# A retention layer with a feed-forward stage: one more load and cast buffer, and the first score group moved to the end of the previous head pair

## The chip, the cores and the metric

The kernel runs on one core of one Trainium2 chip. The time is device microseconds of one execution on that core, and the median of several executions is compared. The engines named below are PE (TensorE: matmuls, transposes and, as "PEld", their weight loads), DVE (VectorE), ACT (ScalarE), SP (SyncE, which here only issues DMAs) and POOL (GpSimd, which here does four memsets at the start).

## What is computed

The input is q, k and v of 4 batches, 8 heads, 768 positions and 64 channels, in fp32, and two weight matrices of 512 x 2048 and 2048 x 512.

```python
gamma = 1.0 - 2.0 ** (-5.0 - np.arange(H))
for t in range(S):
    state = gamma * state + einsum('bhd,bhe->bhde', k[:, :, t], v[:, :, t])
    y[:, :, t] = scale * einsum('bhd,bhde->bhe', q[:, :, t], state)
x = y.transpose(0, 2, 1, 3).reshape(B * S, H * D)
h = x @ w_in
g = h * tanh(log1p(exp(h)))
out = g @ w_out
```

The recurrence over positions is done in chunks of 128: inside a chunk with masked scores, across chunks with a 64 x 64 state for each head.

## The kernel before

There are two stages, one after the other. The first is the retention ("attention" in the names), for 16 head pairs: 4 batches times 4 pairs of heads, `it` = 0 to 15. The second is the feed-forward stage (lines 229 to 264), for 12 blocks of 256 tokens. The retention leaves its result in SBUF, in `xt`, where the second stage reads it.

For one head pair the first stage does this (the letters are used in the rest of the text):

- load: six DMAs of 192 KB, q, k and v of each head (lines 112, 115, 118), into a buffer set of the pool `rn_aload`, which has 3 sets. For the first eight pairs a weight DMA of 1 MB follows each load (`weight_piece`, lines 90 and 96). All DMAs are issued by SP.
- casts, on ACT: qp and kd for the first head, qp and kd for the second head (lines 131 and 134, fp32 to fp16 with a scale), then kb and vb for both heads (lines 137 and 138). They go to the pool `rn_acast`, which has 2 sets.
- QT and KT, on PE: six transposes of qp (line 142) and six of kb (line 144), each followed by a copy from PSUM to SBUF on DVE (lines 148 and 149).
- S.0 and S.1, on PE: the scores of chunks 0 to 2 and of chunks 3 to 5, six matmuls each (line 179), into one PSUM tile `at2`, of which there is a single buffer. AM.0 and AM.1, on DVE: the product of that tile with the mask (line 183).
- for each of the six chunks c: u (line 197, the chunk's k-v product), Y.c (line 199, masked scores times v), t.c (lines 202 and 205, the state's part of the result, one matmul for each head) on PE, and st.c on DVE (line 210, the new state). The result tile `yt_ps` in PSUM holds three chunks and has a single buffer.
- xt.0 after chunk 2 and xt.1 after chunk 5, on ACT: two copies each (lines 216 and 220) that bring `yt_ps` to SBUF. Y of the next three chunks can't start before the second of them has read the tile.

In the source, the loop body issues the load for pair `it`+2, then a weight piece, then casts, QT and KT for pair `it`+1, then everything else for pair `it`. The order on each engine's queue is not that of the source: when the kernel is built, a scheduler places the instructions on the queues by costs of its own, and what it makes is fixed before the run. Each engine then takes its instructions strictly in that order. After the fourth and the eighth weight piece, ACT casts a whole weight matrix to fp16 (lines 92 and 98).

The second stage computes, for each block, `hT` by 64 matmuls (line 242, copied out at line 246), Exp, Ln and Tanh on ACT (lines 249 to 251), the product `gt` on DVE (line 253) and the output by 32 matmuls (line 257), which go out by line 261 and a DMA.

Of the kernel before, what the change touches and what calls it, by code (L numbers as in the profile page):

```python
# [9 lines left out]
FP16 = mybir.dt.float16  # L10
FP32 = mybir.dt.float32
AF = mybir.ActivationFunctionType
ALU = mybir.AluOpType
# [3 lines left out]
def kernel(  # L17
# [9 lines left out]
    nc = tc.nc  # L27
# [3 lines left out]
    P = 128  # L31
    C = 128
    NCH = S // C
    HP = H // 2
# [37 lines left out]
    msk = cpool.tile([P, H, C], FP32)  # L72
# [9 lines left out]
    with tc.tile_pool(name="rn_wstage", bufs=1) as wstage:  # L82
      wtmp = wstage.tile([P, NBP, d_ff], FP32)
      wtmp2 = wstage.tile([P, NFB, d_model], FP32)
      win_ap = moe_w_in.rearrange("(bp p) f -> p bp f", p=P)
      wout_ap = moe_w_out.rearrange("(fb p) c -> p fb c", p=P)

      def weight_piece(j):
          if j < NBP:
              nc.sync.dma_start(wtmp[:, j], win_ap[:, j])  # L90
              if j == NBP - 1:
                  nc.scalar.copy(win16, wtmp)  # L92
          elif j < NBP + 4:
              jj = j - NBP
              fsl = slice(jj * (NFB // 4), (jj + 1) * (NFB // 4))
              nc.sync.dma_start(wtmp2[:, fsl], wout_ap[:, fsl])
              if jj == 3:
                  nc.scalar.copy(wout16, wtmp2)

      with tc.tile_pool(name="rn_aload", bufs=3) as lpool, \  # L100
         tc.tile_pool(name="rn_acast", bufs=2) as castp, \
         tc.tile_pool(name="rn_atp", bufs=2) as tpp, \
         tc.tile_pool(name="rn_asmall", bufs=3) as smallp, \
         tc.tile_pool(name="rn_apsum", bufs=1, space=bass.MemoryType.PSUM) as aps:

        def load(b, hp):
            hA = 2 * hp
            q2 = lpool.tile([P, NCH, 2, D], FP32, tag="q2")
            k2 = lpool.tile([P, NCH, 2, D], FP32, tag="k2")
            v2 = lpool.tile([P, NCH, 2, D], FP32, tag="v2")  # L110
            for hh in range(2):
                nc.sync.dma_start(
                    q2[:, :, hh],
                    q[b, hA + hh].rearrange("(c p) d -> p c d", p=P))
                nc.sync.dma_start(
                    k2[:, :, hh],
                    k[b, hA + hh].rearrange("(c p) d -> p c d", p=P))
                nc.sync.dma_start(
                    v2[:, :, hh],
                    v[b, hA + hh].rearrange("(c p) d -> p c d", p=P))  # L120
            return q2, k2, v2

        def prep(b, hp, loaded):
            hA = 2 * hp
            q2, k2, v2 = loaded
            qp2 = castp.tile([P, NCH, 2, D], FP16, tag="qp2")
            kb2 = castp.tile([P, NCH, 2, D], FP16, tag="kb2")
            vb2 = castp.tile([P, NCH, 2, D], FP16, tag="vb2")
            kd2 = castp.tile([P, NCH, 2, D], FP16, tag="kd2")
            for hh in range(2):  # L130
                nc.scalar.activation(  # L131
                    qp2[:, :, hh], q2[:, :, hh], AF.Copy,
                    scale=dvec[:, hA + hh:hA + hh + 1])
                nc.scalar.activation(
                    kd2[:, :, hh], k2[:, :, hh], AF.Copy,
                    scale=kdv[:, hA + hh:hA + hh + 1])
            nc.scalar.mul(kb2[:], k2[:], BOOST)
            nc.scalar.mul(vb2[:], v2[:], BOOST)
            qt_ps = aps.tile([P, S], FP16, tag="qt_ps")
            kt_ps = aps.tile([P, S], FP16, tag="kt_ps")  # L140
            for c in range(NCH):
                nc.tensor.transpose(  # L142
                    qt_ps[:, c * C:(c + 1) * C], qp2[:, c], ident)
                nc.tensor.transpose(  # L144
                    kt_ps[:, c * C:(c + 1) * C], kb2[:, c], ident)
            qt = tpp.tile([P, S], FP16, tag="qt")
            kt = tpp.tile([P, S], FP16, tag="kt")
            nc.vector.tensor_copy(qt, qt_ps)  # L148
            nc.vector.tensor_copy(kt, kt_ps)  # L149
            return qt, kt, vb2, kd2  # L150

        NIT = B * HP
        loads = [load(0, 0), load(0, 1)]
        pre = prep(0, 0, loads[0])
        for it in range(NIT):
            b, hp = divmod(it, HP)
            hA = 2 * hp
            qt, kt, vb2, kd2 = pre
            if it + 2 < NIT:
                nb, nhp = divmod(it + 2, HP)  # L160
                loads.append(load(nb, nhp))
            weight_piece(it)
            if it + 1 < NIT:
                nb, nhp = divmod(it + 1, HP)
                pre = prep(nb, nhp, loads[it + 1])
            tstate = smallp.tile([P, P], FP16, tag="tstate")
            nc.vector.memset(tstate, 0.0)
            HCH = NCH // 2
            yt_ps = None
            mskb = msk[:, hA:hA + 2].unsqueeze(2).broadcast_to(  # L170
                (P, 2, HCH, C))

            def qk_mask_group(g):
                at2 = aps.tile([P, 2, 4, C], FP32, tag="at2")
                for cc in range(HCH):
                    cs_ = slice((g * HCH + cc) * C, (g * HCH + cc + 1) * C)
                    for hh in range(2):
                        o = 64 * hh
                        nc.tensor.matmul(  # L179
                            at2[:, hh, cc], kt[o:o + 64, cs_],  # L180
                            qt[o:o + 64, cs_], start=True, stop=True)
                am = smallp.tile([P, 2, HCH, C], FP16, tag="atm")
                nc.vector.tensor_tensor(  # L183
                    am, at2[:, :, 0:HCH], mskb, op=ALU.mult)
                return am

            atm3 = qk_mask_group(0)
            atm3_next = None
            for c in range(NCH):
                cs = slice(c * C, (c + 1) * C)  # L190
                g, cc = divmod(c, HCH)
                if cc == 0:
                    yt_ps = aps.tile([P, HCH, 2, C], FP32, tag="yt_ps")
                if cc == 1 and g + 1 < NCH // HCH:
                    atm3_next = qk_mask_group(g + 1)
                u_ps = aps.tile([P, P], FP32, tag="u_ps", bufs=2)
                nc.tensor.matmul(
                    u_ps, kd2[:, c], vb2[:, c], start=True, stop=True)
                nc.tensor.matmul(  # L199
                    yt_ps[:, cc], vb2[:, c], atm3[:, :, cc],  # L200
                    start=True, stop=True)
                nc.tensor.matmul(  # L202
                    yt_ps[0:64, cc, 0], tstate[0:64, 0:64], qt[0:64, cs],
                    start=False, stop=True, skip_group_check=True)
                nc.tensor.matmul(  # L205
                    yt_ps[64:128, cc, 1], tstate[64:128, 64:128],
                    qt[64:128, cs], start=False, stop=True,
                    skip_group_check=True)
                tnew = smallp.tile([P, P], FP16, tag="tstate")
                nc.vector.scalar_tensor_tensor(  # L210
                    tnew, tstate, gcc[:, hp:hp + 1], u_ps,
                    op0=ALU.mult, op1=ALU.add)
                tstate = tnew
                if cc == HCH - 1:
                    c0 = c - HCH + 1
                    nc.scalar.copy(  # L216
                        xt[0:64, b, hp, c0 * C:(c + 1) * C].rearrange(
                            "p (c i) -> p c i", i=C),
                        yt_ps[0:64, :, 0])
                    nc.scalar.copy(  # L220
                        xt[64:128, b, hp, c0 * C:(c + 1) * C].rearrange(
                            "p (c i) -> p c i", i=C),
                        yt_ps[64:128, :, 1])
                    atm3 = atm3_next

    ntok = 0
    GF = 4
    with tc.tile_pool(name="rn_mh", bufs=2) as mhp, \
# [4 lines left out]
        for b in range(B):  # L233
            for cb in range(NCB):
                ts_all = slice(cb * CB, (cb + 1) * CB)
                hT = mhp.tile([P, NFB, CB], FP32)
                for gg in range(NFB // GF):
                    h4 = mps.tile([P, GF, CB], FP32, tag="h4", bufs=3)
                    for j in range(GF):
                        fb = gg * GF + j  # L240
                        for bp in range(NBP):
# [3 lines left out]
                                start=(bp == 0), stop=(bp == NBP - 1))  # L245
# [51 lines left out]
```

## Time and profile before

| what | value |
|---|---|
| median of 6 runs | 392.64 us (391.7 to 395.03) |
| the profiled execution | 393.51 us |
| its span, from the first to the last instruction | 391.7 us |
| mean granted TensorE clock over the span | 0.943 |
| first stage, from the start to the last xt copy | 0 to 170.86 us |
| second stage | 170.9 us to the end |
| first KT transposes of pair 0, 1, 2, 3 | 11.82, 20.56, 29.32, 40.84 us |
| first KT transposes of pair 10, 11, 12, 13, 14, 15 | 118.31, 125.98, 134.83, 144.14, 152.97, 161.73 us |
| weight casts on ACT (lines 92 and 98) | 7.0 us each, at 64.43 and 108.49 us |

The profiled execution lies 0.87 us above the median of the runs. A row of the "windows" view gives a stretch of the span in us, its length, the busy time of PE, PEld, DVE, ACT and POOL in it (with the number of instructions), the granted TensorE clock, the busy share of the DMA engines (as the view gives it; it can exceed 1) and the GB/s moved. A row of the timeline gives start, duration, engine, line, operation and tiles, and in brackets the idle time before it with what ended it. Buffer numbers in names (qp_359) tell the instances of a tile apart.

### The profile page before, as it was taken

Reading aid. Unit: us, or ns where it says so; the run is one execution under the profiler, and the core shown is the slowest. Engines: PE = TensorE matmul, PEld = TensorE weight load, DVE = VectorE, ACT = ScalarE, POOL = GpSimd, SP = SyncE. Lnnn points to the kernel's source line nnn. Section 1 sums busy time; section 2 is a strip of 40 time slices with the busy share of each in tenths; the row PEclk is TensorE's granted clock in tenths of the full one; section 3 lists DMA queues with packets and bytes.
Section 4 is the critical chain, followed back from the end, with each engine's and each line's share of the span. In section 5 each row is a group of like instructions: output and inputs, shape, how many; then the busy total and the mean of one; then the engine's idle time right before and its main releaser. Section 6 shows DMA issues by size and latency. Waiting matters only on the chain.

```text
span 391.7 us, 4763 instructions
## 1 busy us (share of the span) xinstructions
PE 299.1 (76%) x1920; PEld 172.8 (44%) x1920; DVE 204.9 (52%) x260; ACT 265.1 (68%) x223; POOL 0.2 (0%) x4
## 2 busy tenths in 40 slices
PE   0686666576658887889569979979996996995666
PEld 0342333233224444458426756564682665463222
DVE  0454444363445665527267485565837656483351
ACT  2664448855498765415993995799499399849920
POOL 0000000000000000000000000000000000000000
PEclk9999999999999999999959989998996998799589
DMA  8999999983458810000001101000010110001011
GB/s 172 218 278 261 289 266 245 258 210 80 92 122 173 169 23 0 2 0 2 0 0 55 54 2 54 33 22 28 27 55 0 54 55 0 28 36 44 2 54 54
DMA packets 82149, 34.43 MB, mean 88 GB/s; under 512 B 76368, under 2 KB 76368, under 8 KB 81616
## 3 DMA queue, kind: packets, MB, share of 16 engines
q1 hardware_dynamic: 82128, 34.13, 36.4%
q8 instruction: 15, 0.25, 0.3%
q14 instruction: 6, 0.05, 0.0%
HBM read 27.83 MB, written 6.29 MB: 87 GB/s over the span
## 4 chain that ended last, share of the span: by engine, by line
ACT 36%; PE 33%; DVE 19%; issue 6%; DMA 4%; SPq 1%; ACTq 1%; DVEq 0%
PE o_ps L257 12%; DVE gt L253 11%; ACT wt L250 7%; ACT ut L249 7%; PE yt_ps L199 7%; ACT ut L251 6%; PE yt_ps L202 5%; ACT L251 3%; ACT L250 3%; PE kt_ps L144 3%; DVE am L183 3%; ACT xt L220 2%; DVE hT L246 2%; DMA v_351<-in_v_dram 2%; DVE tnew L210 1%
## 5 line engine op out<-in xcount | busy, mean ns | idle before, releaser
L257 PE MATMUL o_ps<-wout_69,gt 128*128 128x512 f16 x384 | 100.9, 429 | 31.2 <-DVE gt L253 31.2
L242 PEld LDWEIGHTS <-win_68 128*128 128x128 f16 x768 | 75.8, 99 | 12.8 <-issue 0.9
L257 PEld LDWEIGHTS <-gt 128*128 128x128 f16 x384 | 40.8, 109 | 88.4 <-DVE gt L253 34.0
L249 ACT ACTIVATE ut<-hT 128x4096 f32<-128x4096 f32 x12 | 43.3, 3610 | 43.1 <-DVE hT L246 43.1
L253 DVE TENSOR_TENSOR gt<-hT,ut 128x4096 f16<-128x4096 f32 x12 | 53.1, 4422 | 22.9 <-ACT ut L251 22.9
L216 ACT CAST xt<-yt_ps 64x384 f16<-64x384 f32 x32 | 15.1, 472 | 57.2 <-PE yt_ps L205 57.0
L210 DVE SCALAR_TENSOR_TENSOR tnew<-tnew,gcc,u_ps 128x128 f16<-128x128 f16 x80 | 27.6, 345 | 34.2 <-PE yt_ps L205 19.9
L261 DVE TENSOR_SCALAR osb<-o_ps 128x512 f32<-128x512 f32 x24 | 16.6, 691 | 53.8 <-PE o_ps L257 53.8
L250 ACT ACTIVATE wt<-ut 128x4096 f32<-128x4096 f32 x12 | 43.4, 3618 | 0.1
L251 ACT ACTIVATE ut<-wt 128x4096 f32<-128x4096 f32 x12 | 43.4, 3617 | 0.1
L148 DVE COPY qt<-qt_ps 128x768 f16<-128x768 f16 x16 | 8.9, 557 | 37.6 <-PE qt_ps L142 37.6
L202 PE MATMUL yt_ps<-qt,tnew 64*64 64x128 f16 x80 | 25.0, 313 | 0.0
L205 PE MATMUL yt_ps<-qt,tnew 64*64 64x128 f16 x80 | 24.9, 312 | 0.0
L202 PEld LDWEIGHTS <-tnew 64*64 64x64 f16 x80 | 10.1, 126 | 30.0 <-issue 28.0
L250 ACT ACT_TABLE_LOAD x12 | 15.4, 1283 | 0.2
L251 ACT ACT_TABLE_LOAD x12 | 15.4, 1283 | 0.2
L220 ACT CAST xt<-yt_ps 64x384 f16<-64x384 f32 x32 | 15.1, 473 | 0.4
L149 DVE COPY kt<-kt_ps 128x768 f16<-128x768 f16 x16 | 8.9, 558 | 10.6 <-PE kt_ps L144 10.5
L179 PEld LDWEIGHTS <-kt 64*128 64x128 f16 x192 | 7.9, 120 | 12.8 <-DVE kt L149 10.6
L205 PEld LDWEIGHTS <-tnew 64*64 64x64 f16 x80 | 9.9, 124 | 0.0
L142 PE MATMUL qt_ps<-ident,qp_109 128*128 128x128 f16 x6 | 0.8, 310 | 10.2 <-ACT qp_109 L131 10.2
L92 ACT CAST win_68<-wtmp 128x8192 f16<-128x8192 f32 x1 | 7.0, 7001 | 0.0
(363 smaller groups left out, 419.4 us busy)
## 6 DMA issues: line engine op xcount, KB each, us to landing
out_dram<-osb SPq DMA_DIRECT2D x24, 256.0 KB, 2.0
wtmp<-in_moe_w_in_dram SPq DMA_DIRECT2D x4, 1024.0 KB, 6.3
wtmp_75<-in_moe_w_out_dram SPq DMA_DIRECT2D x4, 1024.0 KB, 6.9
msk<-rn_msk SPq DMA_DIRECT2D x1, 512.0 KB, 3.5
q_91<-in_q_dram SPq DMA_DIRECT2D x2, 192.0 KB, 4.0
k_92<-in_k_dram SPq DMA_DIRECT2D x2, 192.0 KB, 4.3
v_93<-in_v_dram SPq DMA_DIRECT2D x2, 192.0 KB, 4.4
q_100<-in_q_dram SPq DMA_DIRECT2D x2, 192.0 KB, 4.6
```

Source lines behind the costliest of these rows:

```text
L199: nc.tensor.matmul(yt_ps[:, cc], vb2[:, c], atm3[:, :, cc], start=True, stop=True)
L202: nc.tensor.matmul(yt_ps[0:64, cc, 0], tstate[0:64, 0:64], qt[0:64, cs], start=False, stop=True, skip_group_check=True)
L205: nc.tensor.matmul(yt_ps[64:128, cc, 1], tstate[64:128, 64:128], qt[64:128, cs], start=False, stop=True, skip_group_check=True)
L210: nc.vector.scalar_tensor_tensor(tnew, tstate, gcc[:, hp:hp + 1], u_ps, op0=ALU.mult, op1=ALU.add)
L220: nc.scalar.copy(xt[64:128, b, hp, c0 * C:(c + 1) * C].rearrange("p (c i) -> p c i", i=C), yt_ps[64:128, :, 1])
L242: nc.tensor.matmul(h4[:, j], win16[:, bp, fb * P:(fb + 1) * P], xt[:, b, bp, ts_all], start=(bp == 0), stop=(bp == NBP - 1))
L249: nc.scalar.activation(ut, hT, AF.Exp, scale=inv_boost3)
L250: nc.scalar.activation(wt, ut, AF.Ln, bias=1.0, scale=1.0)
L251: nc.scalar.activation(ut, wt, AF.Tanh)
L253: nc.vector.tensor_tensor(gt, hT, ut, op=ALU.mult)
L257: nc.tensor.matmul(o_ps, gt[:, fb, tsl * P:(tsl + 1) * P], wout16[:, fb], start=(fb == 0), stop=(fb == NFB - 1))
L261: nc.vector.tensor_scalar(osb, o_ps, inv_boost3, None, op0=ALU.mult)
```

## The change

It does three things. The pool of loads has 4 sets, not 3, and the pool of casts 3, not 2. The loads run three pairs ahead, not two, and the casts are a function of their own that runs two pairs ahead, while the transposes stay one pair ahead. S.0 and AM.0 of the next pair are issued at the end of a pair's body, not at the start of the next body. No instruction is added or taken away, and every instruction keeps its shape.

```diff
-      with tc.tile_pool(name="rn_aload", bufs=3) as lpool, \
-         tc.tile_pool(name="rn_acast", bufs=2) as castp, \
+      with tc.tile_pool(name="rn_aload", bufs=4) as lpool, \
+         tc.tile_pool(name="rn_acast", bufs=3) as castp, \
...
-        def prep(b, hp, loaded):
+        def casts(b, hp, loaded):
...
+            return qp2, kb2, vb2, kd2
+
+        def prep(casted):
+            qp2, kb2, vb2, kd2 = casted
...
-        loads = [load(0, 0), load(0, 1)]
-        pre = prep(0, 0, loads[0])
+        loads = [load(*divmod(i, HP)) for i in range(min(3, NIT))]
+        casted = [casts(*divmod(i, HP), loads[i]) for i in range(min(2, NIT))]
+        pre = prep(casted[0])
+        atm3_pre = qk_mask_group(0, pre[0], pre[1], 0)
         for it in range(NIT):
...
+            atm3 = atm3_pre
+            if it + 3 < NIT:
+                loads.append(load(*divmod(it + 3, HP)))
             if it + 2 < NIT:
-                nb, nhp = divmod(it + 2, HP)
-                loads.append(load(nb, nhp))
+                casted.append(casts(*divmod(it + 2, HP), loads[it + 2]))
             weight_piece(it)
             if it + 1 < NIT:
-                nb, nhp = divmod(it + 1, HP)
-                pre = prep(nb, nhp, loads[it + 1])
+                pre_next = prep(casted[it + 1])
...
-            atm3 = qk_mask_group(0)
...
+            if it + 1 < NIT:
+                atm3_pre = qk_mask_group(
+                    2 * ((it + 1) % HP), pre_next[0], pre_next[1], 0)
+                pre = pre_next
```

The scheduler makes of it the following. On SP a weight piece stands one load later (load 3 before weight piece 0, and so on). ACT's queue, with the pair number in brackets and the score group or head after a dot:

```
before, casts of pair 3:  xt(1.1) xt(2.0, first copy) qp(3) xt(2.0, second) kd(3) xt(2.1) qp kd kb vb(3)
after, casts of pair 3:   xt(1.1) qp kd(3) xt(2.0) qp kd kb vb(3) xt(2.1)
before, from the cast of line 98:
  wout  qp kd qp kd kb vb(10)  xt(9.0)  qp kd(11)  xt(9.1)  qp kd kb vb(11)
  qp(12) xt(10.0) kd(12) xt(10.1) qp kd kb vb(12)
  xt(11.0) qp kd(13) xt(11.1) qp(13) xt(12.0) kd kb vb(13) ...
after, from the cast of line 98:
  wout  qp kd qp kd kb vb(11)  qp kd(12)  xt(10.0)  qp(12) xt(10.1, first) kd kb vb(12) xt(10.1, second)
  qp(13) xt(11.0, first) kd(13) xt(11.0, second) xt(11.1) qp kd kb vb(13)
  xt(12.0) qp kd(14) xt(12.1) xt(13.0, first) qp(14) xt(13.0, second) kd kb vb(14) ...
```

PE's queue in the changed program between KT(11) and KT(14) (in the program before, KT(10) to KT(13) holds the same amount of work):

```
KT(11) u S.0(11) Y.3-5(10) QT(12) S.1(11) u u KT(12)
u Y.0-2(11) S.0(12) u u u Y.3-5(11) S.1(12) u u Y.0-2(12) with QT(13) before its last t, u u KT(13)
u u S.0(13, four of six) Y.3-5(12) S.0(13, two) u S.1(13, three) Y.0(13) S.1(13, three) Y.1-2(13) u u QT(14) Y.3-5(13) KT(14)
```

Up to KT(2), and from KT(14) on, the two programs have the same order on PE; the second stage's order is the same on every engine.

## The prediction

> **What bounds the kernel now.** First the page's parts 1 and 4: no engine is busy all the time, and the chain that ended last passes from engine to engine. DMA holds 4% of it.
>
> ```profile
> PE 299.1 (76%) x1920; PEld 172.8 (44%) x1920; DVE 204.9 (52%) x260; ACT 265.1 (68%) x223; POOL 0.2 (0%) x4
> ...
> ACT 36%; PE 33%; DVE 19%; issue 6%; DMA 4%; SPq 1%; ACTq 1%; DVEq 0%
> ```
>
> Then the windows view, cut from the first KT transpose of one pair to that of the next. Pairs differ, so I cost the change interval by interval.
>
> ```profile
> 20.55:29.31 8.76, 6.88 (x50) 3.59 (x48) 4.92 (x12) 5.60 (x11) 0.00 (x0) 1.00 1.25 286
> 29.31:40.84 11.53, 7.23 (x50) 3.46 (x49) 5.19 (x12) 6.00 (x13) 0.00 (x0) 1.00 0.99 274
> ...
> 63.84:74.25 10.41, 5.51 (x40) 2.76 (x40) 4.50 (x10) 10.41 (x8) 0.00 (x0) 1.00 1.17 298
> 74.25:84.95 10.70, 8.99 (x58) 4.32 (x59) 5.68 (x14) 7.22 (x13) 0.00 (x0) 1.00 0.92 232
> ...
> 118.31:125.98 7.67, 6.24 (x44) 3.30 (x45) 4.31 (x10) 6.79 (x12) 0.00 (x0) 1.00 0.85 180
> 125.98:134.83 8.85, 7.60 (x54) 3.85 (x53) 5.26 (x13) 5.83 (x11) 0.00 (x0) 1.00 0.74 156
> 134.83:144.14 9.31, 8.55 (x59) 4.21 (x58) 6.00 (x15) 5.66 (x11) 0.00 (x0) 1.00 0.41 83
> ...
> 152.97:161.73 8.76, 6.88 (x49) 3.58 (x50) 4.92 (x12) 5.60 (x11) 0.00 (x0) 1.00 0.01 2
> ```
>
> There are four kinds. A short interval (8.76) has the next pair's casts inside the current pair's work. A long one (11.5) has them behind it. A weight interval (10.4) holds a 7.0 us weight cast, and a catch-up (10.7, and the three from 118.31) follows it. The clock is 1.00 throughout.
>
> Are the long intervals a DMA wait, which deeper prefetch would remove? The timeline of ACT and SP says no. Pair 3's second q load was issued at 21.47, and its median time to landing is 6.5 us (page, part 6), so it was there by about 31 (24.6 + 6.8 at the latest). The cast qp_359 ran at 35.00, straight behind an xt copy that had waited 4.21 us for PE. It stood behind that copy in the queue.
>
> ```profile
> 21.47 3.12 SPq L112 DMA_DIRECT2D q_243<-in_q_dram  x1
> ...
> 34.63 0.47 ACT L216 CAST xt<-yt_ps 64x384 f16<-64x384 f32 x1 [4.21 <-PE yt_ps L205]
> 35.00 0.61 ACT L131 ACTIVATE qp_359<-q_243,dvec 128x384 f16<-128x384 f32 x1
> ```
>
> So stage one runs at the pace of queue order: PE waits for xt copies, masks and late casts. Stage two is a chain of ACT, DVE and PE that starts when stage one ends.
>
> **Buffers and loads: 0 us.** Load 3 no longer has weight piece 0 ahead of it (0.95 us of SP from 18.41), so it would be issued from 18.41 to 23.7 (six issues of 0.89, as loads 1 and 2 took) and land by about 30, and its first cast would stand behind xt(1.1), which ends at 30.4. From then on a load with its weight piece takes SP 8.2 us (19.36 to 27.28, 36.50, 44.57), less than any interval, so loads gain on the casts. Six loads with four weight pieces are through by 50 and the fourth piece lands by 57 (6.3 us), while the cast of line 92 would start at about 73. The eighth piece follows load 10, whose set comes free with pair 6's casts (about 72), and lands by about 87; the cast of line 98 would start at 117. If that cover were gone, a late weight piece would cost what it is late. The third cast set removes waits only where a cast waited for PE: the trace shows one idle gap of 0.22 us (kd at 128.21), part of the old catch-up that I replace whole below.
>
> **The intervals: one short one moves.** By the two built orders, the changed program begins with three short intervals (0 to 3), then three long (3 to 6), weight, catch-up, two long, weight (10 to 11), then a catch-up of three, and one short (14 to 15). Before it was two short, three long, weight, catch-up, two long, weight (9 to 10), a catch-up of three, and two short. So KT(11) comes one short interval after the old KT(10): 118.31 + 8.76 = 127.07. The gain at pair 3 (11.53 to 8.76) is given back because a long interval follows one pair later and a short one at the end is lost. All other intervals cancel but for the catch-up: old 7.67 + 8.85 + 9.31 = 25.83, new unknown.
>
> **The new catch-up.** I follow its queue order with link durations from the old one. Rows used: PE's Y and t of one chunk 0.57; from Y.0 to the xt copy behind t.2 1.81 (120.03 to 121.84); from the second xt copy to the next Y 0.53 (119.50 to 120.03); ACT steps qp or kd 0.51, kb 0.73, xt copy 0.49; six transposes 0.65 to 0.7, from their start to the DVE copy 0.86; that copy to the next st 0.47, AM to the next DVE operation 0.88, AM to Y or S 1.01.
>
> - KT(11) to KT(12), 6.3: ACT ends the casts of pair 11 at 0.6, then does qp and kd(12) before xt(10.0) (1.6). Y.3(10) follows at 2.6, three chunks, xt(10.1) at 4.45, kd and kb(12) by 5.5, and KT(12) 0.87 behind kb's start.
> - KT(12) to KT(13), 10.7: QT's copy and st delay AM.1(11) to 6.1, st behind it to 7.0, u and Y.0(11) to 7.5. Three chunks, xt(11.0) at 9.3 with kd(13) between its two copies: second at 10.3, Y.3(11) at 10.85. Again 1.81 + 0.49 + 0.53: Y.0(12) at 13.7. Three chunks less the last t, QT(13) at 15.1, its copy and st to 16.9, u, KT(13) at 17.0.
> - KT(13) to KT(14), 10.7: u, copy of kt at 17.9, S.0(13) at 18.5, cut after four by three chunks of pair 12 (1.72), the last two at 20.5, AM.0 at 20.7, S.1 behind it at 21.7, three chunks with the rest of S.1 (2.0) to 23.7, xt(13.0) at 24.1, qp(14) behind it, QT(14) 0.66 later at 25.2, 0.7 and three chunks with a u (1.84): 27.7.
>
> New 27.7 against old 25.83: three pairs, the same PE work, more waits. The largest are Y.3(11) behind an xt copy with a cast in it (0.96), S.1(13) behind a mask that was split off late (1.0), and QT(14) behind qp(14), itself behind xt(13.0) (1.3). Each link is read to 0.05 us or so, and some thirty are chained; I give the sum 27.3 to 28.1.
>
> **Moving S.0 and AM.0: 0 us of its own.** The same 32 masks and score groups run. In a short or long interval S.0 still stands behind KT and its copy (0.61 us, 12.68 to 13.29 in the timeline) in both built orders, because there is one `at2` and S.0 needs KT anyway. Its only effect is in the catch-up above.
>
> The row at 35.00 shows the data landed and the cast waiting for its turn on ACT. The page "Perfetto Trace Analysis" of the Trainium skill ("Optimization Strategy") says that the same gap repeated on the engine that should be busy can mean that there is not enough SBUF or PSUM for the next tile. By that rule, with the added sets, the five long intervals would shrink to short ones, 5 x 2.74 = 13.7 us less, and the sum below would be 380.7; by the row it stays.
>
> **Sum.** From old KT(10) to the last xt copy: before 170.86 - 118.31 = 52.55. After: 8.76 (to KT(11)) + 27.7 + 8.76 + 9.13 (the last pair, 161.73 to 170.86) = 54.35. Difference +1.8 us. Stage two has the same order and starts 1.8 us later. Span 391.7 + 1.8 = 393.5; the profiled execution, 1.8 more than its span, 395.3; it lay 0.87 above the median, so the median becomes 392.64 + 1.8 = 394.4 (+0.46%).
>
> **Rivals.**
>
> *The clock of stage two, slower by over 0.5%.* The output blocks of 32 matmuls start after 2 to 3 us of idle PE and run below full clock; the windows view gives
>
> ```profile
> 264.94:273.72 8.78, 8.78 (x34) 3.73 (x35) 4.18 (x4) 8.74 (x4) 0.00 (x0) 0.81 0.09 31
> 297.93:307.85 9.92, 9.92 (x34) 4.02 (x35) 4.18 (x4) 8.81 (x4) 0.00 (x0) 0.71 0.07 26
> ```
>
> Five such blocks lie on the chain: two at 8.78, two at 9.92, the last at 8.38. A shifted start can put one more in the slow form: +1.14, so 394.4 + 1.1 = 395.5. For: the runs of before spread over 3.3 us with nothing in stage one to vary them. Against: the same spread hits both medians. It decides once one more block of the median run is slow.
>
> *The prefetch does what its name says, faster.* If data were late after all, the five long intervals would become short: 5 x 2.74 = 13.7 less, 392.64 - 13.7 + 1.8 = 380.7; one of them alone gives 391.7. Against: the row at 35.00 and the unchanged queue order. It decides if casts in the changed kernel follow directly on xt copies of the previous pair.
>
> *The catch-up's waits are covered, no slower.* If the three named waits (0.96 + 1.0 + 1.3 = 3.3) lie beside other work, the catch-up is 24.4, 1.4 below the old one: 391.2. For: old PE was busy 22.4 of 25.83 there. Against: each waiter is next in its queue.
>
> **How the numbers follow.** Two medians of a few runs tell about 0.5%, or 1.96 us, from no change. Forecast 0.68, with its own range 393.2 to 395.6; clock 0.17; waits covered 0.09; prefetch 0.06. The forecast's +1.8 lies just inside the bound; its working and the spread of medians put 0.33 above and 0.35 inside. Slower: 0.33 + 0.17 = 0.50; same: 0.35 plus 0.04 of the covered waits, 0.39; faster: 0.05 + 0.06 = 0.11. The range takes in the clock above and most of the covered waits below: 391.9 to 396.4.
>
> **What would show it.** Right: KT(3) at about 38.1, KT(11) at about 127.1, KT(14) at about 154.8, last xt copy at about 172.7; long intervals between pairs 3 and 6 and 8 and 10 still at 11.5; PE's wait for `xt L220` and `am L183` not smaller. Wrong: long intervals below 11, a cast that waits for a DMA, KT(11) to KT(14) outside 27.3 to 28.1, or stage two's length changed by more than 1.2 us.

## The result, and the profile after

The changed kernel took 395.63 us at the median of 10 runs, the old one 392.05 us over 20 runs: ratio 1.0079, 95% interval [1.0052, 1.0106], or 3.1 us slower. (The ratio is that of the means; the medians lie 3.58 us apart.) Two more comparisons of the same pair gave 1.0050 [1.0009, 1.0091] and 1.0049 [1.0015, 1.0083], about 2.0 us. The forecast was 394.4 us, 1.8 us above the old median of 392.64, a ratio of 1.0046: inside the intervals of the two later comparisons, just below that of the first.

Parts 1 and 4 of the page of the changed kernel, in the columns that were shown of the old one:

```profile
PE 298.7 (76%) x1920; PEld 172.3 (44%) x1920; DVE 204.9 (52%) x260; ACT 264.8 (67%) x223; POOL 0.2 (0%) x4
...
ACT 37%; PE 30%; DVE 18%; issue 5%; SPq 4%; DMA 3%; ACTq 1%; DVEq 0%
```

The busy times are those of before to 0.5 us: the same instructions, in a span of 393.4 in place of 391.7 us. The windows view, cut from the first KT transpose of pair 2 on (the clock column reads 0.50 in this profile; the last section comes back to it):

```profile
29.10:37.86 8.76, 6.88 (x51) 3.59 (x49) 4.92 (x12) 5.60 (x11) 0.00 (x0) 0.50 1.02 250
37.86:49.38 11.52, 7.23 (x50) 3.45 (x48) 5.18 (x12) 5.98 (x13) 0.00 (x0) 0.50 1.09 256
...
126.85:133.15 6.30, 4.84 (x37) 2.53 (x37) 3.19 (x8) 5.03 (x10) 0.00 (x0) 0.50 0.90 182
133.15:143.64 10.49, 9.20 (x60) 4.38 (x60) 6.24 (x15) 7.28 (x14) 0.00 (x0) 0.50 0.01 2
143.64:154.59 10.95, 8.99 (x59) 4.30 (x59) 6.08 (x15) 5.95 (x11) 0.00 (x0) 0.50 0.00 1
```

Pair 2 to 3, 11.53 before, is now a short interval, and the long ones follow one pair later at their old length. The three rows from 126.85 are the new catch-up: 6.30 + 10.49 + 10.95 = 27.74, where the old one took 25.83. Stage one ends at 172.53, 1.68 later than before (170.85), and the rest of the span has its old length: 393.4 - 172.5 = 220.9 against 391.7 - 170.9 = 220.8.

ACT's timeline shows where the short interval comes from:

```profile
29.72 0.47 ACT L226 CAST xt<-yt_ps 64x384 f16<-64x384 f32 x1
30.22 0.62 ACT L131 ACTIVATE qp_280<-q_165,dvec 128x384 f16<-128x384 f32 x1
...
34.41 0.47 ACT L222 CAST xt<-yt_ps 64x384 f16<-64x384 f32 x1 [3.06 <-PE yt_ps L211]
```

Pair 3's first cast, which ran at 35.00 behind a wait for PE, runs at 30.22 ahead of that wait. Then the catch-up, PE's timeline first and ACT's below it:

```profile
137.71 0.37 PE L205 MATMUL yt_ps<-am,vb_1131 128*128 128x256 f16 x1 [0.42 <-ACT xt L226]
...
148.53 0.37 PE L165 MATMUL at_1578<-qt,kt 64*128 64x128 f16 x3 [0.83 <-DVE am L169]
152.13 0.82 PE L146 MATMUL qt_ps<-ident,qp_1444 128*128 128x128 f16 x6 [0.76 <-ACT qp_1444 L131]
```

```profile
136.18 0.47 ACT L222 CAST xt<-yt_ps 64x384 f16<-64x384 f32 x1 [1.22 <-PE yt_ps L211]
136.56 0.61 ACT L134 ACTIVATE kd_1342<-k_1226,kdv 128x384 f16<-128x384 f32 x1
137.18 0.47 ACT L226 CAST xt<-yt_ps 64x384 f16<-64x384 f32 x1
...
151.08 0.47 ACT L222 CAST xt<-yt_ps 64x384 f16<-64x384 f32 x1 [2.83 <-PE yt_ps L211]
151.46 0.61 ACT L131 ACTIVATE qp_1444<-q_1330,dvec 128x384 f16<-128x384 f32 x1
```

These are the three waits that the prediction named. At 136.56 a cast of pair 13 sits between the two xt copies that Y.3 of pair 11 waits for. At 148.53 a score group waits for a mask. At 152.13 QT(14) waits for qp(14), which ACT holds behind an xt copy.

### The profile page after: what moved, and what is told of

It is laid out like the page before. It is cut to its first block, busy times and chain, and to the rows that moved or that the text cites. A ratio compares the mean times of both kernels' runs of the same rounds, so it can differ in the third digit from the quotient of the medians.

```text
span 393.4 us, 4761 instructions
## 1 busy us (share of the span) xinstructions
PE 298.7 (76%) x1920; PEld 172.3 (44%) x1920; DVE 204.9 (52%) x260; ACT 264.8 (67%) x223; POOL 0.2 (0%) x4
## 3 DMA queue, kind: packets, MB, share of 16 engines
HBM read 27.83 MB, written 6.29 MB: 87 GB/s over the span
## 4 chain that ended last, share of the span: by engine, by line
ACT 37%; PE 30%; DVE 18%; issue 5%; SPq 4%; DMA 3%; ACTq 1%; DVEq 0%
PE o_ps L267 12%; DVE gt L263 11%; ACT wt L260 7%; ACT ut L259 7%; ACT ut L261 6%; PE yt_ps L205 6%; PE yt_ps L208 5%; ACT L261 3%; ACT L260 3%; DVE am L169 2%; SPq L112 2%; PE kt_ps L148 2%; ACT xt L226 2%; DVE hT L256 2%; ACT wout_69 L98 2%
## 5 line engine op out<-in xcount | busy, mean ns | idle before, releaser
L165 PEld LDWEIGHTS <-kt 64*128 64x128 f16 x192 | 7.7, 117 | 13.5 <-DVE kt L153 10.2
L146 PE MATMUL qt_ps<-ident,qp_118 128*128 128x128 f16 x6 | 0.8, 307 | 10.7 <-ACT qp_118 L131 10.7
```

## The experiments

In the expectations, quoted below, the queue-order theory is the forecast; the prefetch theory and the clock theory are two of its rivals.

### The changed kernel again (e1, e11)

No edit.

> The changed kernel once more, beside the old one on the same chip. Queue-order theory: stage one ends 1.7 us later than in the old kernel (172.5 against 170.9 in the profile) and stage two keeps its length, so +1.7 us (+0.43%) at the median. Clock theory (a later start puts more output blocks of stage two in their slow form): the median is 3 us or more above the old one while stage one still ends at 172.5, so stage two is longer by 1.3 us at the median of the runs.

> The changed kernel a third time, on whatever chip comes. Queue-order theory: ratio 1.0044 to 1.005 (1.7 to 2.0 us of stage one). Clock theory: 1.008 again.

Ratios 1.0050 [1.0009, 1.0091] and 1.0049 [1.0015, 1.0083]. Stage one ended at 172.91 and 172.89, 2.0 us after the old one; the first KT started 0.2 us later (12.00 and 12.06 against 11.82), so from there stage one took 160.91 and 160.83 us against 159.03, 1.8 to 1.9 more. The catch-up in e1, windows view:

```profile
127.25:133.53 6.28, 4.82 (x36) 2.52 (x37) 3.17 (x8) 5.02 (x10) 0.00 (x0) 1.00 0.88 182
133.53:144.02 10.49, 9.20 (x60) 4.39 (x60) 6.25 (x15) 7.28 (x14) 0.00 (x0) 1.00 0.01 2
144.02:154.97 10.95, 8.99 (x59) 4.30 (x59) 6.08 (x15) 5.95 (x11) 0.00 (x0) 1.00 0.00 1
```

The three lengths repeat to 0.02 us. Both ratios are what stage one alone gives (2.0 of 393 is 0.5%). The 1.0079 of the first comparison did not come back, but it lies inside both intervals, so these runs don't exclude it.

### The parts of the change, one by one (e2, e3, e5)

e2 takes the loads back to two ahead and keeps the casts two ahead:

```diff
-      with tc.tile_pool(name="rn_aload", bufs=4) as lpool, \
+      with tc.tile_pool(name="rn_aload", bufs=3) as lpool, \
...
-            if it + 3 < NIT:
-                loads.append(load(*divmod(it + 3, HP)))
             if it + 2 < NIT:
+                loads.append(load(*divmod(it + 2, HP)))
                 casted.append(casts(*divmod(it + 2, HP), loads[it + 2]))
```

> Only the casts move two pairs ahead, with their third set; loads stay two ahead with three sets; the first score group is issued at the end of a pair as in the change. Queue-order theory: the same two short, three long intervals at the start as in the old kernel, then the new catch-up of 27.5 us, so stage one ends at 172.5 and the time is that of the full change. Prefetch theory (the load buffers are what matters): the time of the old kernel.

e3 adds only the load buffer and the third load in advance to the old kernel:

```diff
-      with tc.tile_pool(name="rn_aload", bufs=3) as lpool, \
+      with tc.tile_pool(name="rn_aload", bufs=4) as lpool, \
...
-            if it + 2 < NIT:
-                nb, nhp = divmod(it + 2, HP)
+            if it + 3 < NIT:
+                nb, nhp = divmod(it + 3, HP)
                 loads.append(load(nb, nhp))
```

> Only the loads run three ahead, with four sets; casts, cast sets and first score group as in the old kernel. Queue-order theory: three short intervals at the start, the old catch-up of 25.8 us one pair later, one short interval less at the end: stage one ends at 170.9 as before, ratio 1.000. Prefetch theory: at least the time of one long interval less, 2.7 us faster.

e5 keeps of the change only the moved score group:

```diff
-      with tc.tile_pool(name="rn_aload", bufs=4) as lpool, \
-         tc.tile_pool(name="rn_acast", bufs=3) as castp, \
+      with tc.tile_pool(name="rn_aload", bufs=3) as lpool, \
+         tc.tile_pool(name="rn_acast", bufs=2) as castp, \
...
-            if it + 3 < NIT:
-                loads.append(load(*divmod(it + 3, HP)))
             if it + 2 < NIT:
-                casted.append(casts(*divmod(it + 2, HP), loads[it + 2]))
+                loads.append(load(*divmod(it + 2, HP)))
             weight_piece(it)
             if it + 1 < NIT:
+                casted.append(casts(*divmod(it + 1, HP), loads[it + 1]))
                 pre_next = prep(casted[it + 1])
```

> Only the first score group and its mask are issued at the end of the previous pair; loads two ahead with three sets, casts one ahead with two sets as in the old kernel. Queue-order theory: the scheduler makes the same queues as for the old kernel, so every interval keeps its length, stage one ends at 170.9 and the ratio is 1.000. If moving the group has a worth or a price of its own, the intervals between pairs change by up to the mask's 0.95 us each.

| kernel | ratio to the old kernel | stage one ends | its catch-up |
|---|---|---|---|
| e2, casts ahead | 1.0051 [1.0022, 1.0081] | 172.76 | 6.29 + 10.50 + 10.94 = 27.73 |
| e3, loads ahead | 1.0007 [0.9974, 1.0041] | 170.84 | 7.58 + 8.85 + 9.37 = 25.80 |
| e5, score group moved | 0.9990 [0.9949, 1.0031] | 171.18 (started 0.34 later) | 25.82 |

The whole price is in the casts two pairs ahead with their third set. e2 has it without any deeper load and with the old two short intervals at the start; e3 has the third short interval, loses one at the end, and gains nothing. The moved score group changes no interval. In e3 all five long intervals are still there with the loads one pair earlier; the first of pairs 3 to 6 and the last of pairs 8 to 10, from the windows view:

```profile
38.16:49.69 11.53, 7.24 (x51) 3.46 (x49) 5.20 (x12) 6.01 (x13) 0.00 (x0) 1.00 1.16 256
...
105.22:116.71 11.49, 7.28 (x48) 3.44 (x48) 4.95 (x12) 5.61 (x11) 0.00 (x0) 1.00 0.51 104
```

### The changed kernel with two cast sets (e6)

```diff
-         tc.tile_pool(name="rn_acast", bufs=3) as castp, \
+         tc.tile_pool(name="rn_acast", bufs=2) as castp, \
```

> The changed kernel with two cast sets in place of three; loads three ahead, casts two ahead in the source. Queue-order theory: the first eleven intervals as in the change, but the casts of the catch-up can't run so far ahead of the xt copies; followed by its queue order the catch-up is 26.4 us in place of 27.7 (old: 25.8), so stage one ends at 171.4, 0.6 us over the old one. If the third set is of no account: 172.6 as with the change.

Ratio 0.9974 [0.9934, 1.0014]. The windows view of its catch-up:

```profile
127.56:133.85 6.29, 4.83 (x37) 2.52 (x37) 3.19 (x8) 5.03 (x10) 0.00 (x0) 1.00 0.89 183
133.85:143.69 9.84, 9.24 (x61) 4.36 (x61) 6.17 (x14) 7.01 (x13) 0.00 (x0) 1.00 0.01 2
143.69:153.85 10.16, 9.04 (x60) 4.48 (x59) 6.11 (x15) 6.15 (x12) 0.00 (x0) 1.00 0.00 1
```

26.29, where 26.4 was expected and the change has 27.74. Stage one ended at 171.77 because its first KT started 0.55 us late (12.37); from there it took 159.40 us, against 159.03 in the old kernel and 160.91 in e1. So 1.5 of the change's 1.9 us hang on the third cast set: with it the scheduler lets casts run further ahead of the xt copies. (In the change, a cast of pair 13 stands between the two copies of xt(11.0), as shown above at 136.56; in e6 it follows both, at 137.91.)

### A later start of stage two alone (e4)

```diff
+                    if it == NIT - 1 and c == NCH - 1:
+                        for _ in range(4):
+                            nc.scalar.copy(
+                                xt[64:128, b, hp, c0 * C:(c + 1) * C].rearrange(
+                                    "p (c i) -> p c i", i=C),
+                                yt_ps[64:128, :, 1])
```

> The old kernel with the very last xt copy done five times (four extra copies of 0.49 us on ACT between the stages; same result). It moves stage two by 1.95 us and changes nothing else. Queue-order theory: +1.95 us (+0.5%) at the median. Clock theory: 3 us or more, as with the change.

Ratio 1.0055 [1.0018, 1.0092], as the shift of 1.95 us gives (0.5%). So a later start by itself fits its own length; an effect of up to 3.6 us in all, which the clock theory asks for, is not excluded by the interval. But the profile of e4 has a span of 397.1 us and that of e11 391.6, with stage one ending at 172.81 and 172.89. Three of the output blocks (line 257 of the old kernel) in both, e4 first, from PE's timeline:

```profile
267.65 9.80 PE L263 MATMUL o_ps<-wout,gt 128*128 128x512 f16 x32 [3.29 <-DVE gt L259]
...
335.75 9.88 PE L263 MATMUL o_ps<-wout,gt 128*128 128x512 f16 x32 [3.29 <-DVE gt L259]
...
383.22 10.04 PE L263 MATMUL o_ps<-wout,gt 128*128 128x512 f16 x32 [3.47 <-DVE gt L259]
```

```profile
267.77 7.08 PE L267 MATMUL o_ps<-wout,gt 128*128 128x512 f16 x32 [3.29 <-DVE gt L263]
...
333.23 7.08 PE L267 MATMUL o_ps<-wout,gt 128*128 128x512 f16 x32 [3.29 <-DVE gt L263]
...
379.07 8.73 PE L267 MATMUL o_ps<-wout,gt 128*128 128x512 f16 x32 [4.78 <-DVE gt L263]
```

The same 32 matmuls behind the same idle of 3.29 us take 7.08 or 9.88 us. Up to 268 the two agree to 0.1 us; at the last block they are 4.15 apart. The second stage is the same in both kernels, so this is the spread of several us from run to run, which the forecast had to set beside a change of 1.8.

### The weight pieces off SP's queue (e7, e8, e9, e10)

e7 gives them to GpSimd, with casts of one piece each (the pieces and casts stand at the loop positions `it` and `it - 4`):

```diff
-              nc.sync.dma_start(wtmp[:, j], win_ap[:, j])
-              if j == NBP - 1:
-                  nc.scalar.copy(win16, wtmp)
+              nc.gpsimd.dma_start(wtmp[:, j], win_ap[:, j])
...
+      def weight_cast(j):
+          if 0 <= j < NBP:
+              nc.gpsimd.tensor_copy(win16[:, j], wtmp[:, j])
...
-            weight_piece(it)
+            weight_piece(it - 0)
+            weight_cast(it - 4)
```

> The old kernel with the eight weight pieces issued from GpSimd's queue and cast there piece by piece, so that SP's queue holds loads alone and ACT has no weight cast. Queue-order theory: the scheduler then puts every pair's casts inside the pair before, all fifteen intervals are short (8.76), stage one ends at about 11.8 + 15 x 8.76 + 9.1 = 152.3, and the time falls by 18 us to about 375, if the transfers keep up. Prefetch theory (long intervals wait for data): the loads are as late as before, stage one stays near 170.

Ratio 1.0055 [1.0015, 1.0096], a miss in the time and a hit in the intervals. One of its fifteen, and the start of ACT:

```profile
120.88:129.63 8.75, 6.88 (x51) 3.59 (x49) 4.91 (x12) 5.60 (x11) 0.00 (x0) 1.00 0.65 137
```

```profile
24.08 1.28 ACT L135 ACT_TABLE_LOAD   x1 [24.08 <-DMA q<-in_q_dram]
...
29.48 0.61 ACT L138 ACTIVATE kd<-k,kdv 128x384 f16<-128x384 f32 x1 [3.49 <-DMA k<-in_k_dram]
```

All fifteen intervals lie between 8.72 and 8.76 us: with no weight piece in SP's queue, and the casts in pieces off ACT, there is no long one. But GpSimd issued the weight pieces from 1.24 us on, ahead of the first loads (SP's first from 3.01), and the first KT started at 33.39 in place of 11.8. That the pieces held up the loads is borne out by e9 below, where they are held back. 173.82 - 33.39 = 140.4 us for stage one without its start, against 159.0 before.

e8 issues the pieces from ACT's queue (`nc.scalar.dma_start`, at `it - 2`) and casts them on ACT one by one (`nc.scalar.copy`, at `it - 6`):

> The weight pieces are issued from ACT's queue two pairs later than in the old kernel and cast on ACT piece by piece, four pairs after the issue. Queue-order theory: no long interval is left, and the pieces (1.75 us each) fill ACT's gaps; followed by the queues, intervals of 7 to 9.5 us and stage one ending at 140 to 150, the time at 362 to 372. Three weight pieces go out before the first loads, so the first interval starts later by up to 8 us. Prefetch theory: near 170.

369.97 us, ratio 0.9381 [0.9306, 0.9455]. The first KT started at 18.34 and stage one ended at 147.38, inside what was expected. Its intervals run from 6.10 to 9.72 us, wider than the 7 to 9.5 expected.

e9 holds the pieces back, with the loop positions `it - 3` and `it - 7`:

```diff
+        for j in range(NBP):
+            nc.gpsimd.tensor_copy(wtmp[:, j, 0:1], loads[1][2][:, 0, 0, 0:1])
+            nc.gpsimd.tensor_copy(wtmp2[:, 4 * j, 0:1], loads[1][2][:, 0, 1, 0:1])
```

> As e8, but no weight piece may be issued before the second pair's loads have landed (one element of each piece is written first, from that pair's v, by GpSimd), with three pairs between loop position and issue. Queue-order theory: the first KT starts at 11.9 and not at 18.3, the intervals stay at 7 to 9.5, and stage one ends at 141 to 144: 4 to 6 us less than e8, 362 to 366 us. If the transfers themselves bind (27.3 MB at the 260 GB/s of the old page are 105 us, and a load with a weight piece took 8.2 us), some intervals of 7 stretch to 8.2 and it ends near 146.

364.57 us, ratio 0.9270 [0.9224, 0.9316]: 7.3% below the old kernel, and the best version found. The first KT started at 11.86 and stage one ended at 144.00. From the first KT it took 132.1 us, where e7 took 140.4 with every interval short: intervals of 6.10 to 9.44 us, so a short one (8.75) is not the least that the work needs. Which part of the edit gives these 8 us was not taken apart.

e10 makes the same weight edits on the changed kernel:

> The same weight edits on the changed kernel (loads three ahead, casts two ahead, moved first score group). Queue-order theory: no long interval was left for the prefetch to remove, so within 1 us of e9. Prefetch theory: with the weight pieces out of the way the deeper buffers pay, 3 us or more below e9.

370.61 us, ratio 0.9431 [0.9379, 0.9483]: 6 us above e9. Neither theory had that. What ACT waited for among the loads, e10 first, then e9 (us in total, times, longest), besides one wait of 6.9 us for the first q in both:

```profile
ACT kd L138 <- DMA k<-in_k_dram: 7.4, 8, 2.7
...
ACT qp L135 <- DMA q<-in_q_dram: 4.4, 6, 1.2
ACT vb L142 <- DMA v<-in_v_dram: 1.5, 1, 1.5
```

```profile
ACT qp L135 <- DMA q<-in_q_dram: 4.7, 4, 2.2
...
ACT kd L138 <- DMA k<-in_k_dram: 1.5, 5, 0.5
```

Casts placed two pairs ahead reach the head of ACT's queue before their data has landed (kd 7.4 against 1.5, vb 1.5 against none), and the xt copies behind them wait too. Stage one ended 3.9 us later than in e9 (147.86); the other 2.2 us of the two profiled spans are stage two (221.9 and 219.7). The waits point to the casts; e10 differs from e9 by the whole change, and its parts were not tried one by one here.

## Why the prediction was right

- **Long intervals are queue order, not late data.** Shown: e3 deepens the loads, keeps all five long intervals and gains nothing (1.0007). The old kernel's waits view has no load that ACT waited for after the first pair; these are all:

```profile
ACT L131 <- DMA q_91<-in_q_dram: 6.9, 1, 6.9
ACT kd_112 L134 <- DMA k_92<-in_k_dram: 0.3, 1, 0.3
ACT qp_109 L131 <- DMA q_91<-in_q_dram: 0.3, 1, 0.3
```

  The 6.5 us to landing that the prediction gives stands in the view of DMAs, not on the page. The chain view does put a load (v_351, 6.40 us, to 34.74) ahead of the cast at 35.00. It is no wait: that cast follows its xt copy by 0.37 us (34.63 to 35.00), and those of pairs 4 and 5 do the same (46.13 to 46.50, 57.63 to 58.00) with no load in the chain. e7 takes the weight pieces out of SP's queue and every interval becomes short. That the scheduler expected later data because of the weight pieces is argued from this, not shown; e7 and e8 also cut the weight casts into pieces.
- **Load buffers: 0.** Shown by e3. One step of the working was misread: a load with its weight piece takes SP 7.92, 9.22 and 8.07 us (19.36, 27.28, 36.50, 44.57), so one took more than a short interval. It cost nothing, since in the changed kernel too ACT waited for loads in the first pair alone.
- **One short interval moves.** KT(3) at 37.86 (forecast 38.1), KT(11) at 126.85 in the profile beside the result and 127.25 in e1 (127.1). The first of these profiles comes close by two deviations: its first KT started 0.47 us late (12.29) and one interval, KT(1) to KT(2), was 0.68 us shorter than in e1 (8.08 against 8.76; see the last section).
- **The new catch-up, 27.7.** Measured 27.74, 27.72 and 27.73. Its three links of 6.3, 10.7 and 10.7 came out at 6.30, 10.49 and 10.95, so two errors of 0.2 cancel, by luck. e2 and e6 show that the casts ahead and their third set make it. The waits named in it stand in the timeline, with idle of 0.42, 0.83 and 0.76 where the working had 0.96, 1.0 and 1.3; why the rows show less was not worked out.
- **The moved score group: 0.** Shown by e5.
- **The sum.** +1.8 us of stage one: from the first KT to its end, 1.9 and 1.8 in e1 and e11, 1.2 in the profile beside the result, where the interval of 8.08 is the difference; by the end of stage one alone, 2.0, 2.0 and 1.7. Stage one is what the prediction got right. The median is a weaker witness: it moved by 3.58 us in the first comparison (means 3.1) and by 0.73 and 1.30 in the two others. The first median, 395.63, lies just above the forecast's own range (393.2 to 395.6), at the 395.5 that the clock rival gave. For that rival's mechanism there is no sign in the profile beside the result, whose stage two kept its length (220.9 against 220.8), and the surplus was not reproduced; the intervals of e1, e11 and e4 don't exclude it, and its cause stays open beyond the spread of stage two.
- **Mis-sized: the clock rival.** It priced one more slow block at 1.14 us, the step between two slow forms. The blocks were seen at 7.08 to 10.04 us, so one more costs up to 2.8 (9.92 - 7.08), and stage two took 218.7 to 224.3 us in the profiles with its old order. A change of stage two by more than 1.2 us, one of the signs of being wrong, therefore tells little in a single profile.
- **PE's waits** behaved as named: for xt copies they rose (10.2 to 11.3 us in total), for masks they stayed (8.7, then 8.0 behind Y and the 0.8 of S.1 at 148.53).
- **The rule on repeated gaps.** "Optimization Strategy" of "Perfetto Trace Analysis" allows that such gaps mean too few buffers. Here more load buffers (e3) left all five gaps, and another queue for the weights (e7) removed them without a buffer.

## What to carry to other kernels

Where a scheduler fixes the queues at build time, compare the built order before you cost a deeper buffer: a cast that stood behind a copy in its engine's queue stayed late however early its data landed (e3). Work hoisted ahead on a queue can delay what is queued behind it (e2, 1.9 us), and more so where it must also wait for its own data (e10, by its waits). Look for what the order is bent around: here taking eight weight transfers out of the load queue and cutting their casts into pieces gave 7.3% (e9), and deeper buffers gave nothing.

## What the hardware did unexpectedly

In the profile beside the result the granted clock stands at 0.50 from 25.4 us to just past 175; in e1, with the same program, it is 1.00 there. The intervals are the same to 0.02 us (10.49 and 10.95 in both), so in stage one the same lengths stand beside both records. One stretch shows that stage one's matmuls can run faster than that. The interval from KT(1) to KT(2) in the profile beside the result, and the one from KT(2) to KT(3) in e1 (from KT(1) to KT(2) e1 took 8.76 us as well, 20.73 to 29.49):

```profile
21.02:29.10 8.08, 5.96 (x51) 3.34 (x49) 4.85 (x12) 5.60 (x11) 0.00 (x0) 0.77 1.19 270
```

```profile
29.49:38.25 8.76, 6.88 (x50) 3.59 (x49) 4.91 (x12) 5.60 (x11) 0.00 (x0) 1.00 1.07 226
```

The interval with the lower record is the shorter one. In it, at 24.07, 24.73 and 25.12, just before the record falls, the three matmuls of Y take 0.28 us each. The other 93 of that profile, and all 96 of e1, take 0.37 to 0.42. So a record of 1.00 stands beside both lengths, and it can't be read as full speed in stage one: the prediction's "the clock is 1.00 throughout" quotes the record and does not say how fast the matmuls ran. The start of stage two says the same: its first 16 matmuls took 3.37 us at a record of 0.50 in that profile and 3.39 at 1.00 in the old kernel's, the next 16 1.91 in both. The forecast used no term from the clock in stage one. The page "TensorE: Matmul & The Clock Gate" ("Seeing it yourself") warns that such records have been unreliable on this chip; these rows agree. What set off the fast stretch no run shows.

In stage two's output blocks the record goes with the length: at 0.71 a block took 9.92 us, at 0.81 8.78, and at 1.00 7.08. The same page ("What's actually happening") says that the clock gate judges activity in windows of 3413 ns that run freely, not from the kernel's start. Idle of 3.29 us before a block, just below that length, followed by 7.08 us in one run and 9.88 in another, fits this; no run here tests it.
